# Two raw query-and-key buffers, later maxima and ten GpSimd pauses in an attention and feed-forward kernel

## The chip, the cores and the metric

One core of one Trainium2 chip runs the whole program. The metric is the device time of one execution in microseconds. On the core, PE (TensorE) multiplies matrices, DVE (VectorE), ACT (ScalarE) and POOL (GpSimd) work on elements, and SP (SyncE) issues the DMA transfers. Each engine does its own instructions strictly in order.

## The reference

```python
def _attn_ref(q_l, k_l, v_l, q_g, k_g, v_g):      # batch 8, heads 8, 512 local + 32 global tokens, head_dim 64
    window, scale = 32, 1.0 / np.sqrt(D)
    k_all = np.concatenate([k_g, k_l], axis=2)
    v_all = np.concatenate([v_g, v_l], axis=2)
    out_g = np.matmul(sm(scale * np.matmul(q_g, k_all.transpose(0, 1, 3, 2))), v_all)
    s_ll = scale * np.matmul(q_l, k_l.transpose(0, 1, 3, 2))
    s_ll = np.where(np.abs(pos[:, None] - pos[None, :]) <= window, s_ll, -1000000000.0)
    s_lg = scale * np.matmul(q_l, k_g.transpose(0, 1, 3, 2))
    out_l = np.matmul(sm(np.concatenate([s_lg, s_ll], axis=-1)), v_all)
    return np.concatenate([out_g, out_l], axis=2)

def _moe_ref(x, w_in, w_out):                     # 4608 tokens x 512, d_ff 2048
    h = x @ w_in
    g = h * np.cos(h)
    return g @ w_out
```

`sm` is the softmax over the last axis; the attention's output, tokens by 512, is x. Everything is float32 in and out.

## The kernel before

**Planes.** The matmuls take float16. A float32 operand is scaled by a power of two, found from its largest magnitude, and kept as two float16 planes, a high one (the rounded value) and a low one (what is left). A product is three matmuls: high by high, high by low, low by high.

**Attention** runs by batch b (0 to 7) and pair p of heads (0 to 3). Batches 0 and 1 have a path of their own; batches 2 to 7 take these steps for a pair:

- `load_qk` (L505): SP loads the pair's raw queries and keys, 608 KB, into the tile `qkr`, of which there is one buffer.
- `qk_a`, `qk_b`, `qk_c`: DVE finds the largest magnitude `qm` (L584) and puts it on a diagonal `d_qk` (L560); PE spreads it over the partitions (`pm_qk`, L566); DVE makes the scale `qs` (L571) and the factor `al` (L603) of it.
- `qk_d`: ACT writes the high plane `qa` (L624), DVE the low plane `kl` (L625, 128x1216). After `kl` the buffer of `qkr` is free.
- `qk_e`: SP moves halves of the planes to where PE wants them (`kh` L634 and L635, `qa` L637, `kl` L639).
- scores: PE `ps` (L879, L880); DVE adds the mask and finds the minimum (`t` and `mn`, L896, one custom instruction, which also frees the PSUM buffer); ACT takes Exp (L484); DVE the sums' reciprocals `sm` (L915, L916); POOL normalizes `t` (L926) and makes the low plane `plx` (L931).
- SP transposes `plx` to `ptb` (L936), PE multiplies by the values (`acc`, L968), and ACT and DVE write the result's planes `xh` and `xl` (L987, L988). The global tokens have the like (`gps`, `gt`, `planes_g`, `gacc`).

Values go by batch: `load_v` (L553, 1280 KB into `vr`, one buffer), `v_a` (DVE `vm`, L653, one reduce over 128x2560, and a diagonal `d_v`), `v_b` and `v_c` (`pm_v` on PE, the scale on DVE), and by pair `v_d` (the planes `vhl`, ACT L682 and DVE L683).

**The feed-forward** runs in 16 chunks c of 256 tokens (two to a batch) and one of all global tokens, in 8 slots j each. For a slot: `m1_a` puts h into a PSUM tile `ph` (PE, L1126, three buffers); `m1_b` and `m1_c` reduce the angle (`u`, ACT L1148 and DVE L1149) and take the sine (ACT); `m1_d` squares it on POOL (`w`, L1163), multiplies by h on DVE (`gf`, L1165, which frees `ph`), and makes the planes `gh` (ACT, L1169) and `gl` (POOL, L1170); `m2_a` multiplies by w_out into `po` (PE, L1184 to L1186). After slot 7 `m2_b` writes `o` from `po`, one half on ACT and one on DVE (L1192), and `m2_c` stores it. `gh` and `gl` lie in a ring of `NG` = 11 buffers.

**The order.** Steps are put into lists by slot (`at`, 16 slots to a batch, offsets such as `s_load` and `s_vd`), and a scheduler orders each engine's instructions from there; `tc.add_manual_dep` adds a dependence that it must keep, with a semaphore (`sync`) or in the order alone (`order`).

```python
t = 16 * (b - 1) + T0[b > 2] + SH
tv = max(t + s_v, 19)
at(tv, PA0, load_v, b)
at(tv + 1, PF, v_a, b)
at(tv + (1 if b == 2 else 2), PG if b == 2 else PA, v_b, b)
at(tv + (1 if b == 2 else 2), PG2 if b == 2 else PB, v_c, b)
```

Of the kernel before, what the change touches and what calls it, by code (L numbers as in the profile page):

```python
# [15 lines left out]
ALU = mybir.AluOpType  # L16
AX = mybir.AxisListType
# [34 lines left out]
LAG = 6  # L52
NG = 11
MASK = -(2.0**120)
# [53 lines left out]
s_tr = -1  # L108
s_vd = -8
s_av = 0  # L110
# [36 lines left out]
def body(tc, qk, qkf, v, wi, wo, mask, out):  # L147
# [3 lines left out]
    with ExitStack() as ctx:  # L151
# [15 lines left out]
        planes = [plx[:, i] for i in range(4)]  # L167
        vhl = cp.tile([P, 2, 5, NT, P], F16, name="vhl")
        vhlf = vhl.rearrange("p a b c d -> p (a b c d)")
# [320 lines left out]
        def load_qk(b, p):  # L490
            if b in FB:
                if p > 0:
                    tag = ("qa", "kh", "kl")[p - 1]
                    q, k = (ap_.tile([P, NZ], F32, tag=tag, name=f"{n}f_{b}_{p}") for n in "qk")
                else:
                    t = ap_.tile([P, 2, NZ], F32, tag="qkr", name=f"qkr_{b}_{p}", bufs=1)
                    q, k = t[:, 0], t[:, 1]
                st["qkf", b, p] = (q, k)
                if b:
                    load_half(b, p, 0, NZ)  # L500
                else:
                    load_half(b, p, 0, ZH)
                return
            t = ap_.tile([P, 2, NZ], F32, tag="qkr", name=f"qkr_{b}_{p}", bufs=1)
            nc.sync.dma_start(t, qk[b, p])  # L505
            st["qkr", b, p] = t

        def h_load(b, p):
            if p > 0:
                tag = ("qa", "kh", "kl")[p - 1]  # L510
                q, k = (ap_.tile([P, NZ], F32, tag=tag, name=f"{n}f_{b}_{p}") for n in "qk")
            else:
                t = ap_.tile([P, 2, NZ], F32, tag="qkr", name=f"qkr_{b}_{p}", bufs=1)
# [55 lines left out]
        def scale_of(s, m):  # L569
# [4 lines left out]
            )  # L574

        def qk_a(b, p):
            m = ap_.tile([P, 1], F32, tag="qm", name=f"qm_{b}_{p}")

            if b < QMA:
                kl = ap_.tile([P, 2, NZ], F16, tag="kl", name=f"kl_{b}_{p}")  # L580
                st["kl", b, p] = kl
                nc.scalar.activation(kl.bitcast(BF16), st["qkr", b, p], AF.Abs, accum_out=m)
            else:
                nc.vector.tensor_reduce(  # L584
                    m, st["qkr", b, p], axis=AX.XY, op=ALU.max, apply_absolute_value=True
                )
            pow2(m, m)
            spread_a(m, 2.0**-40, f"qk{b}_{p}")
# [19 lines left out]
        def qk_d(b, p):  # L608
# [32 lines left out]
        def v_a(b):  # L641
            m = ap_.tile([P, 1], F32, tag="vm", name=f"vm_{b}")
            if b < QMA:
                m4 = ap_.tile([P, 4], F32, tag="vm4", name=f"vm4_{b}", bufs=1)
                for p in range(4):
                    o = 4096 + 640 * (p % 3)
                    nc.scalar.activation(
                        vhlf[:, o : o + 640].bitcast(BF16), st["vr", b][:, p].rearrange("p a b -> p (a b)"),
                        AF.Abs, accum_out=m4[:, p : p + 1],
                    )  # L650
                nc.vector.tensor_reduce(m, m4, axis=AX.X, op=ALU.max)
            else:
# [230 lines left out]
        def sc_b(b, p, i):  # L883
# [272 lines left out]
        def m1_d(c, j):  # L1156
# [319 lines left out]
```

## Time and profile before

| what | value |
|---|---|
| three runs | 1016.23, 1016.11, 1013.29 us; median 1016.11 |
| profiled execution, its own time | 1014.64 us |
| its span, first to last instruction | 1012.9 us |
| mean granted TensorE clock | 0.957 of full |
| busy: PE, DVE, ACT, POOL | 909.4, 652.7, 657.8, 644.5 us |
| chain that ended last, largest shares | PE 37%, POOL 14%, DMA 10%, DVE 9% |

The profile is of one execution. Busy times are sums over the span; a matmul's row can overlap the next one's, and what an engine waited for is inferred from the semaphore that released it. The 1.74 us between the span and its own time lie around the program.

### The profile page before, as it was taken

To read this page: it belongs to the slowest core of one execution; us is meant where nothing else is said; L and a number is where in the kernel's file an instruction comes from. 1 tells how busy PE (TensorE), PEld (TensorE's weight loads), DVE (VectorE), ACT (ScalarE), POOL (GpSimd) and SP (SyncE) were. 2 spreads that over 40 slices of the span, in tenths; PEclk is the share of its full clock that TensorE was granted. 3 is DMA by queue.
4 is the path that set the end of the run, shared out by engine and by line. 5 is a ranking of instruction groups with operands and counts; after the bars stand their busy time and mean duration, and the time that the engine had idled before them with its cause. 6 is when DMAs were issued, how large, how long until landed. Compare 5 with 4: busy or idle time off the path is not lost.

```text
span 1012.9 us, 20948 instructions
## 1 busy us (share of the span) xinstructions
PE 909.4 (90%) x7892; PEld 620.0 (61%) x7892; DVE 652.7 (64%) x1534; ACT 657.8 (65%) x1322; POOL 644.5 (64%) x862
## 2 busy tenths in 40 slices
PE   5659977887999789998999899989989999999996
PEld 4547644455666566765666566666657676666662
DVE  6998698567776777576677658586857553332230
ACT  4669886567788387766686677667767775434440
POOL 3457998745777577867677576747676877344440
PEclk9779995998999899999999999999999999999999
DMA  9684114646754465554546454545464523000000
GB/s 356 237 288 160 54 60 115 116 100 153 148 110 115 103 168 101 105 129 109 107 96 122 119 118 83 123 136 125 92 126 92 101 43 76 1 22 10 13 21 21
DMA packets 162254, 110.79 MB, mean 109 GB/s; under 512 B 140136, under 2 KB 142312, under 8 KB 160232
## 3 DMA queue, kind: packets, MB, share of 16 engines
q1 hardware_dynamic: 162152, 109.44, 43.9%
q8 instruction: 62, 1.02, 0.4%
q14 instruction: 40, 0.33, 0.1%
HBM read 51.61 MB, written 8.91 MB: 60 GB/s over the span
## 4 chain that ended last, share of the span: by engine, by line
PE 37%; POOL 14%; DMA 10%; DVE 9%; ACT 4%; issue 4%; SPq 1%; POOLq 0%; ACTq 0%; DVEq 0%
PE ph L1126 17%; POOL plx L931 6%; PE po L1184 6%; PE po L1186 6%; PE po L1185 5%; POOL t L926 4%; DMA qkr<-qk 4%; DMA vr<-v 2%; DVE kl L625 2%; POOL w L1163 2%; DMA ptb<-plx 2%; ACT t L484 1%; DVE qm L584 1%; POOL gl L1170 1%; PE acc L968 1%
## 5 line engine op out<-in xcount | busy, mean ns | idle before, releaser
L1126 PE MATMUL ph<-xh,wi_h 128*128 128x256 f16 x1024 | 283.3, 278 | 28.2 <-DVE gf L1165 23.6
L1126 PE MATMUL ph<-xl,wi_h 128*128 128x256 f16 x1024 | 283.5, 277 | 0.9 <-DVE xl L805 0.9
L1126 PE MATMUL ph<-xh,wi_l 128*128 128x256 f16 x1024 | 283.5, 277 | 0.0
L1126 PEld LDWEIGHTS <-wi_h 128*128 128x128 f16 x2176 | 213.2, 99 | 78.8 <-issue 33.7
L1170 POOL TENSOR_TENSOR gl<-gf,gh 128x512 f16<-128x512 f32 x136 | 159.9, 1176 | 124.3 <-ACT gh L1169 124.3
L1184 PE MATMUL po<-wo_h,gh 128*128 128x512 f16 x544 | 208.1, 384 | 5.7 <-DVE o L1192 4.9
L1185 PE MATMUL po<-wo_l,gh 128*128 128x512 f16 x544 | 208.1, 383 | 0.7 <-POOL wo_l L236 0.7
L1186 PE MATMUL po<-wo_h,gl 128*128 128x512 f16 x544 | 207.5, 383 | 0.0
L1163 POOL TENSOR_TENSOR w<-w 128x512 f32<-128x512 f32 x136 | 144.5, 1064 | 90.5 <-ACT w L484 90.2
L1149 DVE SCALAR_TENSOR_TENSOR u<-u,cm,ph 128x512 f32<-128x512 f32 x136 | 101.0, 743 | 118.2 <-ACT u L1148 118.0
L1165 DVE SCALAR_TENSOR_TENSOR gf<-w,ph 128x512 f32<-128x512 f32 x136 | 92.9, 683 | 106.5 <-POOL w L1163 106.4
L1169 ACT CAST gh<-gf 128x512 f16<-128x512 f32 x136 | 83.0, 611 | 118.6 <-DVE gf L1165 117.6
L484 ACT ACTIVATE t<-t,mn 128x224 f32<-128x224 f32 (+1 forms) x256 | 117.7, 461 | 58.8 <-DVE mn L896 40.9
L926 POOL TENSOR_TENSOR t<-t,sm 128x192 f32<-128x192 f32 (+1 forms) x192 | 101.9, 563 | 71.1 <-DVE sm L916 71.1
L484 ACT ACTIVATE w<-u,ca 128x512 f32<-128x512 f32 x136 | 97.5, 720 | 63.3 <-DVE u L1149 59.6
L931 POOL TENSOR_TENSOR plx<-t,plx 128x192 f16<-128x192 f32 (+1 forms) x192 | 118.3, 646 | 0.0
L1126 PEld LDWEIGHTS <-wi_l 128*128 128x128 f16 x1088 | 108.1, 99 | 15.5 <-issue 1.3
L1148 ACT ACTIVATE u<-ph,cm 128x512 f32<-128x512 f32 x136 | 92.0, 678 | 23.7 <-PE ph L1126 23.6
L1186 PEld LDWEIGHTS <-gl 128*128 128x128 f16 x544 | 53.7, 99 | 63.9 <-issue 4.1
L1185 PEld LDWEIGHTS <-gh 128*128 128x128 f16 x544 | 53.6, 99 | 60.5 <-issue 11.2
L1184 PEld LDWEIGHTS <-gh 128*128 128x128 f16 x544 | 53.7, 99 | 52.2 <-issue 2.8
L896 DVE CUSTOM_DVE_ANT_0 t<-ps,msk,al 128x192 f32<-128x192 f32 (+1 forms) x192 | 75.6, 427 | 8.1 <-PE ps L880 8.1
(235 smaller groups left out, 1374.0 us busy)
## 6 DMA issues: line engine op xcount, KB each, us to landing
qkr<-qk SPq DMA_DIRECT2D x24, 608.0 KB, 4.7
vr<-v SPq DMA_DIRECT2D x8, 1280.0 KB, 8.4
out<-o SPq DMA_DIRECT2D x34, 256.0 KB, 2.0
kh<-qa SPq DMA_DIRECT2D x48, 152.0 KB, 2.7
wo_h<-wo SPq DMA_DIRECT2D x8, 512.0 KB, 5.2
wo_l<-wo SPq DMA_DIRECT2D x8, 512.0 KB, 5.5
qa<-kl SPq DMA_DIRECT2D x24, 152.0 KB, 3.2
kl<-kl SPq DMA_DIRECT2D x24, 152.0 KB, 3.0
```

The lines of the kernel that those rows point to most:

```text
L484: ins = nc.scalar.activation(*a, **k).ins
L926: nc.gpsimd.tensor_tensor(t[:, h], t[:, h], rb[:, h], op=ALU.mult)
L931: nc.gpsimd.tensor_tensor(lo[:, h], t[:, h], hi[:, h], op=ALU.subtract)
L1126: nc.tensor.matmul(ph[:, a], w[:, kc, f], x[:, kc, q], start=first and ip == 0, stop=last and ip == 2, skip_group_check=True,)
L1148: nc.scalar.activation(u, ph, AF.Identity, bias=m)
L1149: nc.vector.scalar_tensor_tensor(u, u, m, ph, op0=ALU.subtract, op1=ALU.subtract)
L1163: nc.gpsimd.tensor_tensor(w, w, w, op=ALU.mult)
L1165: nc.vector.scalar_tensor_tensor(gf, w, 0.5, st.pop(("ph", c, j)).rearrange("p a b -> p (a b)"), op0=ALU.subtract, op1=ALU.mult,)
L1170: nc.gpsimd.tensor_tensor(gl, gf, gh, op=ALU.subtract)
L1184: nc.tensor.matmul(po[k], gh[:, q], wo_h[:, f], start=(f == 0), stop=False)
L1185: nc.tensor.matmul(po[k], gh[:, q], wo_l[:, f], start=False, stop=False)
L1186: nc.tensor.matmul(po[k], gl[:, q], wo_h[:, f], start=False, stop=(f == NJ - 1))
```

## The change

1. `qkr` has two buffers (the tile pool's default). A dependence in the order alone (`held`) puts `qm` of a pair behind `kl` of the pair before on DVE. Batch 1's raw loads are spread over other tiles (`h_load`).
2. The ring `NG` of `gh` and `gl` has 10 buffers.
3. The value planes `vhl` have four buffers, one to a pair, where there were five, and `s_vd` goes from -8 to -6, so that they are written two slots later.
4. For b > 2 `v_q` takes the place of `v_a`, three slots later: four reduces of 128x640 into `vm4` and one over their results, each held behind a `t` instruction of the last pair of the batch before. `v_b` and `v_c` come three slots later too.
5. `port_gap`: in slot 7 of chunks 2 to 11, POOL's `w` waits on a semaphore for `kl` of pair 2c + 8 (counted over all batches), which is pair 0 or 2 of a batch.

```diff
-NG = 11
+NG = 10
-s_vd = -8
+s_vd = -6
-        vhl = cp.tile([P, 2, 5, NT, P], F16, name="vhl")
+        vhl = cp.tile([P, 2, 4, NT, P], F16, name="vhl")
+        def port_gap(ins, key):
+            if key in st:
+                tc.add_manual_dep(ins, st[key].name, sync, reason="port_gap")
...
 def load_qk(b, p):
-            t = ap_.tile([P, 2, NZ], F32, tag="qkr", name=f"qkr_{b}_{p}", bufs=1)
+            t = ap_.tile([P, 2, NZ], F32, tag="qkr", name=f"qkr_{b}_{p}")
...
 def h_load(b, p):
-            if p > 0:
-                tag = ("qa", "kh", "kl")[p - 1]
-                q, k = (ap_.tile([P, NZ], F32, tag=tag, name=f"{n}f_{b}_{p}") for n in "qk")
+            if p > 1:
+                tags = (("kl", "kl"), ("qa", "kh"))[p - 2]
+                q, k = (ap_.tile([P, NZ], F32, tag=t, name=f"{n}f_{b}_{p}") for n, t in zip("qk", tags))
...
+        def held(ins, key):
+            if key in st:
+                tc.add_manual_dep(ins, st[key].name, order, reason="place")
 def qk_a(b, p):
-                nc.vector.tensor_reduce(
+                ins = nc.vector.tensor_reduce(
                     m, st["qkr", b, p], axis=AX.XY, op=ALU.max, apply_absolute_value=True
-                )
+                ).ins
+                held(ins, ("klins", NPAIR * b + p - 1))
...
+        def v_q(b):
+            m = ap_.tile([P, 1], F32, tag="vm", name=f"vm_{b}")
+            m4 = ap_.tile([P, 4], F32, tag="vm4", name=f"vm4_{b}", bufs=1)
+            for p in range(NPAIR):
+                ins = nc.vector.tensor_reduce(
+                    m4[:, p : p + 1], st["vr", b][:, p], axis=AX.XY, op=ALU.max,
+                    apply_absolute_value=True,
+                ).ins
+                held(ins, ("tins", b - 1, VPIN, p))
+            nc.vector.tensor_reduce(m, m4, axis=AX.X, op=ALU.max)
+            spread_a(m, 2.0**-100, f"v{b}")
...
 def m1_d(c, j):
-            nc.gpsimd.tensor_tensor(w, w, w, op=ALU.mult)
+            ins = nc.gpsimd.tensor_tensor(w, w, w, op=ALU.mult).ins
+            if j == 7 and c > 1:
+                port_gap(ins, ("klins", 2 * c + 8))
...
-            at(tv + 1, PF, v_a, b)
-            at(tv + (1 if b == 2 else 2), PG if b == 2 else PA, v_b, b)
-            at(tv + (1 if b == 2 else 2), PG2 if b == 2 else PB, v_c, b)
+            at(tv + (1 if b == 2 else 2 + 2), PF, v_a if b == 2 else v_q, b)
+            at(tv + (1 if b == 2 else 3 + 2), PG if b == 2 else PA, v_b, b)
+            at(tv + (1 if b == 2 else 3 + 2), PG2 if b == 2 else PB, v_c, b)
```

How instructions move, at three places. The numbers behind a name are batch and pair, or chunk and slot, and last a running number; the change's line numbers are some 5 to 26 higher.

DVE in the second pair of batch 5, before: the maximum of batch 6's values (`vm_6`).

```order
L584 TENSOR_REDUCE qm_5_3_7409<-qkr_5_3_7309 128x1
L206 TENSOR_SCALAR qm_5_3_7409<-qm_5_3_7409 128x1
L560 TENSOR_SCALAR d_qk5_3_7412<-ident_64,qm_5_3_7409 128x128
L1149 SCALAR_TENSOR_TENSOR u_8_1_7344<-u_8_1_7344,cm_8_7239,ph_8_1_7319 128x512
L653 TENSOR_REDUCE vm_6_7881<-vr_6_7707 128x1
L896 ISA t_5_1_2_7304,mn_5_1_3_7402<-ps_5_1_3_7397,msk_73,al_5_1_6711 128x192
L896 ISA mn_5_1_3_7402 128x1
L896 ISA t_5_1_2_7304,mn_5_1_3_7402<-ps_5_1_3_7397,msk_73,al_5_1_6711 128x192
L896 ISA mn_5_1_3_7402 128x1
L988 SCALAR_TENSOR_TENSOR xl_5_7406<-acc_5_0_7360,xs_91,xh_5_7405 128x512
L915 TENSOR_SCALAR sm_5_1_7416<-sm_5_1_7416 128x8
```

DVE in the change, where that maximum now stands, in the last pair of batch 5:

```order
L920 ISA t_5_3_2_8090,mn_5_3_3_8188<-ps_5_3_3_8183,msk_73,al_5_3_7501 128x192
L920 ISA mn_5_3_3_8188 128x1
L920 ISA t_5_3_2_8090,mn_5_3_3_8188<-ps_5_3_3_8183,msk_73,al_5_3_7501 128x192
L920 ISA mn_5_3_3_8188 128x1
L674 TENSOR_REDUCE vm4_6_8194<-vr_6_7721 128x1
L1012 SCALAR_TENSOR_TENSOR xl_5_7420<-acc_5_2_8146,xs_91,xh_5_7419 128x512
L939 TENSOR_SCALAR sm_5_3_8207<-sm_5_3_8207 128x8
L679 TENSOR_REDUCE vm_6_8193<-vm4_6_8194 128x1
L1057 TENSOR_SCALAR gsm_5_1_8216<-gsm_5_1_8216 128x1
L940 RECIPROCAL sm_5_3_8207<-sm_5_3_8207 128x8
L565 TENSOR_SCALAR d_v6_8200<-ident_64,vm_6_8193 128x128
```

The one long reduce stood ahead of the scores of the second pair; the four short ones stand behind the score instructions of the fourth pair (the last of them, `vm4_6`, is shown), and `vm_6` is over four numbers only.

DVE at the start of batch 6, before:

```order
L1015 COPY gal_6_0_8636<-al_6_1_8270 64x1
L1165 SCALAR_TENSOR_TENSOR gf_9_1_8213<-w_9_1_8128,ph_9_1_8102 128x512
L625 SCALAR_TENSOR_TENSOR kl_6_1_8362<-qkr_6_1_8092,qs_6_1_8265,qa_6_1_8361 128x1216
L1149 SCALAR_TENSOR_TENSOR u_9_3_8336<-u_9_3_8336,cm_8_7239,ph_9_3_8311 128x512
L896 ISA t_6_0_1_8357,mn_6_0_1_8358<-ps_6_0_1_8352,msk_73,al_6_0_7847 128x224
L896 ISA mn_6_0_1_8358 128x1
L896 ISA t_6_0_1_8357,mn_6_0_1_8358<-ps_6_0_1_8352,msk_73,al_6_0_7847 128x224
L896 ISA mn_6_0_1_8358 128x1
L1165 SCALAR_TENSOR_TENSOR gf_9_2_8307<-w_9_2_8243,ph_9_2_8217 128x512
L1149 SCALAR_TENSOR_TENSOR u_9_4_8399<-u_9_4_8399,cm_8_7239,ph_9_4_8374 128x512
```

and in the change, from the same `gf_9_1` on:

```order
L1191 SCALAR_TENSOR_TENSOR gf_9_1_8223<-w_9_1_8131,ph_9_1_8105 128x512
L1173 SCALAR_TENSOR_TENSOR u_9_3_8353<-u_9_3_8353,cm_8_7253,ph_9_3_8328 128x512
L707 SCALAR_TENSOR_TENSOR vhl_77<-vr_6_7721,vs_6_8277,vhl_77 128x640 x2
L920 ISA t_6_0_1_8374,mn_6_0_1_8375<-ps_6_0_1_8369,msk_73,al_6_0_7859 128x224
L920 ISA mn_6_0_1_8375 128x1
L1191 SCALAR_TENSOR_TENSOR gf_9_2_8324<-w_9_2_8253,ph_9_2_8227 128x512
L920 ISA t_6_0_1_8374,mn_6_0_1_8375<-ps_6_0_1_8369,msk_73,al_6_0_7859 128x224
L920 ISA mn_6_0_1_8375 128x1
L635 SCALAR_TENSOR_TENSOR kl_6_1_8381<-qkr_6_1_8095,qs_6_1_8282,qa_6_1_8380 128x1216
L593 TENSOR_REDUCE qm_6_2_8556<-qkr_6_2_8452 128x1
L1173 SCALAR_TENSOR_TENSOR u_9_4_8418<-u_9_4_8418,cm_8_7253,ph_9_4_8393 128x512
```

The two `vhl` planes have come in ahead of `kl_6_1`, `kl_6_1` stands one `gf` later than it did, and `qm_6_2` follows it at once, where before it came seven rows behind the last row shown.

POOL at the end of chunk 8, before:

```order
L1163 TENSOR_TENSOR w_8_6_7809<-w_8_6_7809 128x512
L1170 TENSOR_TENSOR gl_8_5_7777<-gf_8_5_7779,gh_8_5_7776 128x512
L931 TENSOR_TENSOR plx_76<-t_5_2_2_7647,plx_76 128x224 x2
L931 TENSOR_TENSOR plx_76<-t_5_2_2_7647,plx_76 128x192 x2
L1163 TENSOR_TENSOR w_8_7_7919<-w_8_7_7919 128x512
L1170 TENSOR_TENSOR gl_8_6_7887<-gf_8_6_7889,gh_8_6_7886 128x512
L1170 TENSOR_TENSOR gl_8_7_8029<-gf_8_7_8031,gh_8_7_8028 128x512
```

and in the change:

```order
L1187 TENSOR_TENSOR w_8_6_7821<-w_8_6_7821 128x512
L1196 TENSOR_TENSOR gl_8_5_7789<-gf_8_5_7791,gh_8_5_7788 128x512
L955 TENSOR_TENSOR plx_76<-t_5_2_2_7661,plx_76 128x224 x2
L955 TENSOR_TENSOR plx_76<-t_5_2_2_7661,plx_76 128x192 x2
L1196 TENSOR_TENSOR gl_8_6_7895<-gf_8_6_7897,gh_8_6_7894 128x512
L1187 TENSOR_TENSOR w_8_7_7927<-w_8_7_7927 128x512
L1196 TENSOR_TENSOR gl_8_7_8032<-gf_8_7_8034,gh_8_7_8031 128x512
L1187 TENSOR_TENSOR w_9_0_8064<-w_9_0_8064 128x512
```

`w_8_7`, which now waits for the low plane of batch 6's first pair (2 x 8 + 8 = 24 = 4 x 6 + 0), has moved behind `gl_8_6`.

On SP the loads of `qkr` stand one pair earlier: those of batch 2's pairs 0 and 1 follow each other, and the load of `vr` comes next; before, that of pair 1 came only behind the moves of pair 0's `kh`. The raw queries and keys of batch 1's first pair are loaded ahead of the pieces of w_out.

## Rows read from the trace of the kernel before

**Rows 1.** Busy time in stretches of the span. Columns: the stretch, its length, busy us (and instructions) of PE, PEld, DVE, ACT and POOL, the granted TensorE clock (1.00 is full), the DMA engines' busy share, GB/s.

```profile
270.00:380.00 110.00, 97.92 (x917) 68.05 (x915) 79.95 (x191) 78.20 (x168) 75.92 (x101) 0.94 0.57 129
380.00:450.00 70.00, 70.00 (x692) 48.35 (x691) 49.86 (x122) 50.01 (x98) 52.21 (x72) 1.00 0.50 98
450.00:773.00 323.00, 302.00 (x2821) 207.82 (x2820) 226.29 (x539) 224.80 (x462) 221.30 (x294) 0.99 0.51 115
```

**Rows 2.** PE's waits between 450 and 773 us by line: what it waited for; us in total, times, longest.

```profile
PE pm_qk L566 <- DVE mn L896: 8.2, 3, 2.9
PE po L1184 <- DVE o L1192: 4.9, 5, 1.9
PE ph L1126 <- DVE gf L1165: 4.2, 9, 0.6
PE gacc L1059 <- DVE mn L896: 2.2, 3, 0.7
PE acc L968 <- DMA ptb<-plx: 1.1, 1, 1.1
```

**Rows 3.** Single starts on PE with a wait before them. Columns of this and the other timelines: start us, duration us, engine, line, operation, out<-in, shape, count, and in brackets the idle time before it and what ended that.

```profile
463.21 0.22 PE L566 MATMUL pm_qk<-d_qk,ones 128*128 128x128 bf16 x1 [2.41 <-DVE mn L896]
...
470.50 0.27 PE L1126 MATMUL ph<-xh,wi_h 128*128 128x256 f16 x1 [0.61 <-DVE gf L1165]
...
488.33 0.38 PE L1184 MATMUL po<-wo_h,gh 128*128 128x512 f16 x1 [1.31 <-DVE o L1192]
```

**Rows 4.** DVE's waits for loads between 380 and 830 us, columns as in the waits above.

```profile
DVE qm L584 <- DMA qkr<-qk: 20.6, 11, 3.4
...
DVE vm L653 <- DMA vr<-v: 3.5, 3, 1.6
```

**Rows 5.** DVE's timeline around a batch's first steps (459 to 488 us).

```profile
459.67 2.82 DVE L653 TENSOR_REDUCE vm<-vr 128x1 f32<-128x2560 f32 x1 [1.13 <-DMA vr<-v]
462.40 0.41 DVE L896 CUSTOM_DVE_ANT_0 t<-ps,msk,al 128x192 f32<-128x192 f32 x1
...
484.96 1.42 DVE L584 TENSOR_REDUCE qm<-qkr 128x1 f32<-128x1216 f32 x1 [2.64 <-DMA qkr<-qk]
...
487.53 0.74 DVE L1192 TENSOR_SCALAR o<-po,co 128x512 f32<-128x512 f32 x1
```

**Rows 6.** The chain of waits between 445 and 490 us, its two loads: start, duration, what.

```profile
451.76 7.88 DMA vr<-v
...
479.77 5.17 DMA qkr<-qk
```

**Rows 7.** SP's timeline (it issues the loads; a row is the issue, not the transfer).

```profile
231.67 0.38 SPq L553 DMA_DIRECT2D vr<-v  x1
...
233.36 0.47 SPq L634 DMA_DIRECT2D kh<-qa  x1
...
235.90 0.35 SPq L505 DMA_DIRECT2D qkr<-qk  x1
```

**Rows 8.** PE's waits between 230 and 380 us, columns as above.

```profile
PE ph L1126 <- DVE gf L1165: 8.0, 4, 5.6
PE ps L879 <- DMA qa<-kl: 5.1, 1, 5.1
PE ps L880 <- DMA kl<-kl: 2.6, 1, 2.6
```

**Rows 9.** The chain of waits between 236 and 262 us, its two transfers: start, duration, what.

```profile
233.88 6.41 DMA kh<-qa
...
240.35 2.35 DMA qa<-kl
```

**Rows 10.** All executions of line 625: count, shortest/median/longest ns, first and last start.

```profile
L625 DVE SCALAR_TENSOR_TENSOR kl<-qkr,qs,qa x24: 1467/1863/8524, 216.0 to 790.8; 128x1216 f16<-128x1216 f32 x24
```

**Rows 11.** DVE's timeline, three of those executions.

```profile
332.79 8.52 DVE L625 SCALAR_TENSOR_TENSOR kl<-qkr,qs,qa 128x1216 f16<-128x1216 f32 x1
...
445.40 4.04 DVE L625 SCALAR_TENSOR_TENSOR kl<-qkr,qs,qa 128x1216 f16<-128x1216 f32 x1
...
470.83 1.86 DVE L625 SCALAR_TENSOR_TENSOR kl<-qkr,qs,qa 128x1216 f16<-128x1216 f32 x1 [0.39 <-ACT qa L624]
```

**Rows 12.** POOL's timeline around the first two of these, and the long run of work at a batch's start.

```profile
338.98 1.05 POOL L931 TENSOR_TENSOR plx<-t,plx 128x192 f16<-128x192 f32 x2
...
443.86 2.20 POOL L931 TENSOR_TENSOR plx<-t,plx 128x224 f16<-128x224 f32 x4
446.01 1.05 POOL L1163 TENSOR_TENSOR w<-w 128x512 f32<-128x512 f32 x1
447.00 1.16 POOL L1170 TENSOR_TENSOR gl<-gf,gh 128x512 f16<-128x512 f32 x1
451.76 1.16 POOL L1170 TENSOR_TENSOR gl<-gf,gh 128x512 f16<-128x512 f32 x1 [3.60 <-ACT gh L1169]
...
464.36 4.36 POOL L926 TENSOR_TENSOR t<-t,sm 128x192 f32<-128x192 f32 x8 [5.95 <-DVE sm L916]
...
480.56 1.04 POOL L1163 TENSOR_TENSOR w<-w 128x512 f32<-128x512 f32 x1
```

**Rows 13.** Busy time in one stretch, columns as in rows 1.

```profile
464.36:481.60 17.24, 16.01 (x122) 10.54 (x121) 10.64 (x28) 12.92 (x25) 17.24 (x23) 1.00 0.59 113
```

**Rows 14.** The page's sixth part: a DMA issue, its engine and count, KB each, us from issue to landing.

```profile
qkr<-qk SPq DMA_DIRECT2D x24, 608.0 KB, 4.7
```

More of the change, by code (lines that the diff above doesn't have):

```diff
@@ L46 @@
 HB = (1,)
+VPIN = 3
 FTE = ((1, 1, 0, 1), (0, 0, 0, 0))
@@ L503, in load_qk @@
                 return
-            t = ap_.tile([P, 2, NZ], F32, tag="qkr", name=f"qkr_{b}_{p}", bufs=1)
+            t = ap_.tile([P, 2, NZ], F32, tag="qkr", name=f"qkr_{b}_{p}")
             nc.sync.dma_start(t, qk[b, p])
@@ L508, in h_load @@
         def h_load(b, p):
-            if p > 0:
-                tag = ("qa", "kh", "kl")[p - 1]
-                q, k = (ap_.tile([P, NZ], F32, tag=tag, name=f"{n}f_{b}_{p}") for n in "qk")
+            if p > 1:
+                tags = (("kl", "kl"), ("qa", "kh"))[p - 2]
+                q, k = (ap_.tile([P, NZ], F32, tag=t, name=f"{n}f_{b}_{p}") for n, t in zip("qk", tags))
             else:
-                t = ap_.tile([P, 2, NZ], F32, tag="qkr", name=f"qkr_{b}_{p}", bufs=1)
+                t = ap_.tile([P, 2, NZ], F32, tag="qkr", name=f"qkr_{b}_{p}")
                 q, k = t[:, 0], t[:, 1]
@@ L624, in qk_d @@
                 nc.scalar.activation(qa, t, AF.Identity, scale=s)
-                nc.vector.scalar_tensor_tensor(kl, t, s, qa, op0=ALU.mult, op1=ALU.subtract)
+                st["klins", NPAIR * b + p] = nc.vector.scalar_tensor_tensor(
+                    kl, t, s, qa, op0=ALU.mult, op1=ALU.subtract
+                ).ins
             kh = ap_.tile([P, 2, NZ], F16, tag="kh", name=f"kh_{nm}")
@@ L645, in v_a @@
                 for p in range(4):
-                    o = 4096 + 640 * (p % 3)
+                    o = 4096
                     nc.scalar.activation(
@@ L655, in v_a @@
                 )
+            spread_a(m, 2.0**-100, f"v{b}")
[6 more added lines that the diff above has]
+                    apply_absolute_value=True,
+                ).ins
+                held(ins, ("tins", b - 1, VPIN, p))
+            nc.vector.tensor_reduce(m, m4, axis=AX.X, op=ALU.max)
             spread_a(m, 2.0**-100, f"v{b}")
@@ L673, in v_d @@
             t, s = st["vr", b], st["vs", b]
-            vh, vl = (vhl[:, i, (NPAIR * b + p) % 5] for i in range(2))
+            vh, vl = (vhl[:, i, p] for i in range(2))
             ve = VE[min(b, 2)]
@@ L895, in sc_b @@
             for h in range(2):
-                nc.vector.tensor_tensor_reduce(
+                st["tins", b, p, i] = nc.vector.tensor_tensor_reduce(
                     t[:, h], pt[:, h], msk[:, MOFF[i] : MOFF[i] + w], al, 3.0e38,
                     ALU.add, ALU.min, mn[:, h : h + 1],
-                )
+                ).ins
             st["t", b, p, i] = (t, mn)
```

## The prediction

> **What bounds the kernel now.** I read the busy times by stretch first. Between 380 and 450 us PE is busy all 70.00 us at full clock, while DVE, ACT and POOL are busy for about 50 each [rows 1]: there the matmuls set the time and the elementwise work fits beside them. The kernel can gain only where PE stands still or is throttled. Between 450 and 773 us PE is busy for 302.00 of 323.00 us [rows 1], so 21.0 us are idle at a granted clock of 0.99. Between 270 and 380 us it is 97.92 of 110.00.
>
> The second view is PE's waits. The five rows of 450 to 773 us sum to 20.6 us, nearly the whole idle time [rows 2]. Largest is `pm_qk`: 8.2 us in three waits, one to each batch start in the stretch. The reader should not stop at the name of the releaser. `pm_qk` needs a PSUM buffer that the score instruction `t` frees; `t` starts at 462.40 because DVE, which works in order, is held by `vm` until then: 1.13 us of waiting for the values' load, then 2.82 us of reducing [rows 5]. PE resumes at 463.21 after 2.41 us [rows 3]. The waits of `po` for `o` have the same form: `o` at 487.53 stands behind `qm` at 484.96, which had waited 2.64 us for its load [rows 5], and PE lost 1.31 us [rows 3].
>
> The third view, DVE's own waits, tells how common this is: `qm` waits 20.6 us in 11 times between 380 and 830 us, `vm` 3.5 us in three [rows 4]. The chain of waits holds both loads, 7.88 and 5.17 us [rows 6]: with one `qkr` buffer a load can only start once `kl` has read the old data.
>
> **The change part by part.** The sum is made against the profiled execution's own 1014.64 us, 1.47 us below the median of the three runs (1016.11). A measurement of this kernel tells about 0.3%, 3 us, from no change.
>
> *1. The maximum of the values.* It leaves the place ahead of the first pairs' scores; four short reduces go behind the last pair's scores. Load wait and reduce no longer stand between PE and a PSUM buffer: **-8.2 us** [rows 2]. The reducing itself stays, 2.82 us a batch, about 0.7 us a piece [rows 5]; a piece could hold up the next `pm_qk` in each of three batches, 3 x 0.7 = 2.1, so the weak end is -6.1. I take the full amount, since DVE has room: 226.29 busy of 323.00 us [rows 1].
>
> *2. The second `qkr` buffer.* A load is issued one pair, about a quarter of a batch, ahead; on SP it waits for `kl` of two pairs before, long done, so nothing queues behind it there. The longest wait of `qm` is 3.4 us [rows 4] and a load takes 4.7 us [rows 14], so a whole pair covers it. What was behind `qm` on DVE gets free: of the 4.9 us of `po` I take **-4.0** (ends 0 and -4.9), since I followed the mechanism through one of the five waits only.
>
> *3. POOL's late start.* At a batch's start POOL idles 5.95 us for `sm`, which comes after `vm` on DVE, then works without a break from 464.36 to 481.60: 17.24 of 17.24 us [rows 12, 13]. `ph` waits for `gf` in such a run, 0.61 us at 470.50 [rows 3]. An earlier `sm` starts the run earlier. Of the row's nine waits I take four of this size, two to a batch start: 4 x 0.6 = **-2.4** (ends 0 and -4.2, the whole row [rows 2]).
>
> *4. The pauses.* `kl` at 445.40 took 4.04 us; the shortest of the 24 took 1.467 [rows 10, 11]. It ended at 449.44, 1.28 us after POOL's `gl` had ended at 448.16; on POOL `plx`, `w` and `gl` had followed each other without a gap [rows 12]. At 332.79 it took 8.52 us, until 1.28 us after POOL's last `plx` of that run (340.03) [rows 11, 12]. So `kl` can stand still for as long as POOL's queue is full, and a pause lets it in. In the steady part a hold of 4.04 - 1.47 = 2.57 us shows no wait on PE of its own: between 380 and 450 us, with 445.40 inside, PE was never idle [rows 1]. There the pause gains nothing. The 8.52 us one cost PE 5.6 us [rows 8]; there the pausing `w` is one of the last instructions of POOL's run, so I take a third, **-1.9** (ends 0 and -5.6). The price: `w` waits up to 1.47 us for `kl`, ten times, 14.7 us at most, and `gf`, `gh` and `gl` queue behind it. I take 0: POOL idled 3.60 us right behind [rows 12], and holds of 2.57 us on DVE, on which the same `gf` stands, cost nothing. That slack is the cover; gone, the ten pauses would cost up to those 14.7.
>
> By the Trainium skill (SBUF — State Buffer, section "SBUF: two separate sides") a DVE operation with two SBUF inputs and GpSimd contend for one port pair, which whichever starts first holds for one whole instruction. By that rule `kl` would get in when the running POOL instruction ends, at most about 1.2 us later. The trace differs: `kl` stood through several ends, and the measurement decides. By the rule, this term and the next would both be near 0, and the sum -16.6 instead of -15.5; it would also strike rival C below.
>
> *5. Batch 3's load.* At 231.67 SP issues the 1280 KB of `vr`, then `kh`, then `qkr` at 235.90 [rows 7]; `kh` needs 6.41 us [rows 9], and PE waits 5.1 us for `qa` and 2.6 us for `kl` [rows 8]. In the change `qkr` goes ahead of these, `vr` stays. One of two competitors leaves: **-2.0** of the 5.1 (ends 0 and -5.1).
>
> *6. What moves into POOL's dense run.* Two `vhl` instructions and the odd pairs' `kl` of five batches now fall into it, where `kl` before mostly got away with 1.86 us [rows 11]. Two holds of up to 2.57 us in five batches are 25.7 us of DVE time. On PE a hold of 2.57 showed 0 and one of 7.05 (8.52 - 1.47) 5.6, so the ends are 0 and 5 x 5.6 = 28. The nearest row is the 2.57 us hold, but in the dense run `gf` is already late by 0.61 [rows 3]; I take one such wait to a batch, 5 x 0.6 = **+3.0**.
>
> *7. At no cost.* The ring of 10: no wait of PE, DVE or POOL in the rows is for a buffer of `gh` or `gl`; with slots of some 6.7 us (323 us in three batches of 16) the one buffer less is one slot of reserve out of eleven. If that cover is gone, `gh` and then POOL wait for `po`. Four `vhl` planes: each is written two slots later, so none waits for its old reader. The batch-1 load ahead of w_out's pieces: one load, 0 to 4.7 us [rows 14], beside work that doesn't need it; I take 0.
>
> Sum: -8.2 - 4.0 - 2.4 - 1.9 - 2.0 + 3.0 = -15.5, so 1014.64 - 15.5 = **999 us**. Next in line are `gacc`'s waits (2.2 us) and what is left of `gf`'s [rows 2].
>
> **The rivals.**
>
> *A, more than the sum.* If all idle time of the steady part goes (20.6), and in the transition 5.6, 5.1 and 2.6 too [rows 2, 8], it is -33.9, 981 us; half of the surplus gives 990. For it: with DVE, ACT and POOL about 70% busy there, nothing else is near its limit [rows 1]. Against: POOL's run stays dense.
>
> *B, the pauses give it back.* The removed waits are worth 15.5, and `w` late ten times by 1.47 us costs 14.7: about 1014. It decides if `ph`'s three buffers are already all in use when the pause comes. For it: `ph` waits for `gf` nine times [rows 2]. Against: those waits lie in the dense run, the pauses at the end of a chunk, before POOL's 3.60 us idle. Here belongs, too, that `kl` misses the pause, because `qa` is late, and POOL waits for nothing.
>
> *C, slower: the moved work is caught by the dense run.* On DVE the two `vhl` and then `kl` come up in the run of 17.24 us. If they are held not for 2.57 us but to the run's end, `gf` stands behind them and PE stops, as behind the 8.52 us `kl`. Five times 5.6 in place of term 6's 3.0 gives 1014.64 - 18.5 + 28 = 1024 us. It loses against before from 18.5 / 5 = 3.7 us on PE a batch; between the two holds known (2.57 us: 0, 7.05 us: 5.6) that is a hold of about 5.5 us. For it: by both rows a full POOL queue holds DVE without limit. Against: the odd `kl` at 470.83 lay in the run and took only 1.86 us [rows 11], so the run has places where it gets in.
>
> **How the numbers follow.** The forecast has a chance of 0.52; its own range is 992 (terms 1 to 4 at their full ends, -22.9, the others 0) to 1007 (term 1 at -6.1, 2 to 5 at half, 6 at +3: -8.2). A has 0.17, B 0.16, C 0.15. The range of 984 to 1014 takes in most of A and all of B's middle, and leaves out C and a little of A and B. Faster by over 0.3% are the forecast, A and a third of B: 0.74. Within 0.3% is most of B: 0.11. Slower is C: 0.15.
>
> **What would show it.** Right: no wait of `qm` for `qkr` and none of `vm` for `vr` on DVE; `pm_qk` gone from PE's waits; PE's idle time over three steady batches down from 21 us to some 7; even pairs' `kl` at about 1.5 us instead of 4.04, with POOL idle before slot 7's `w`. Term 6 is read from the odd `kl` and the first two `vhl` of a batch: about 4 us is the forecast, over 7 us with PE waits of 4 us for `gf` is C. The prediction is wrong if PE's idle time stays at 21 us under other names, or if `ph` waits for `gf` right after each pause (B).

## The result, and the profile after

The changed kernel takes 999.22 us (median of four, 995.87 to 999.53) against 1016.17 of before: 0.9833 of the time, 95% interval 0.9805 to 0.986. The profiled execution took 999.00; 999.0 was forecast. The sum hides two errors of some 6 us that cancel, as this section and the experiments show.

First, where the time went. DVE's `o` of a chunk's second half marks a chunk's end in every profile (its start in the timeline, us):

| chunk | before | change | difference | change, second profile |
|---|---|---|---|---|
| 0 | 185.59 | 187.39 | +1.80 | +2.36 |
| 1 | 231.82 | 237.04 | +5.22 | +5.10 |
| 3 | 374.02 | 375.19 | +1.17 | +0.91 |
| 4 | 432.06 | 435.51 | +3.45 | +3.17 |
| 7 | 594.20 | 587.32 | -6.88 | -7.18 |
| 11 | 805.21 | 789.45 | -15.76 | -16.02 |
| 16 | 1003.70 | 987.92 | -15.78 | -15.90 |

Chunk 2 is left out: its end comes 11 to 20 us later than before in every other kernel of this document, the one with the smaller ring and four planes alone among them, while chunk 3's end is at most 9 us later, so it is no common mark. Up to chunk 4 the change loses 3.4 us, from there to chunk 11 it gains 19.2, and after that nothing. That middle part, called the steady part below, in busy time (columns as in [rows 1]), first before:

```profile
432.06:805.21 373.15, 351.47 (x3288) 241.99 (x3286) 260.10 (x625) 261.16 (x538) 257.67 (x343) 1.00 0.51 112
```

and the changed kernel:

```profile
435.51:789.45 353.94, 346.89 (x3286) 241.21 (x3286) 250.26 (x638) 263.63 (x541) 259.42 (x344) 1.00 0.53 117
```

PE's idle time falls from 21.7 to 7.1 us. All of PE's waits there in the change, to be held against [rows 2]:

```profile
PE po L1210 <- ACT o L1220: 3.5, 3, 1.3
PE acc L992 <- DMA ptb<-plx: 1.7, 2, 1.4
PE ph L1150 <- DVE gf L1191: 1.6, 3, 0.7
PE ps L904 <- DMA kl<-kl: 1.1, 1, 1.1
```

In this stretch the five rows of [rows 2] had 8.2, 4.9, 4.4, 2.2 and 1.4 us before. Those of `pm_qk` and `gacc` are gone, and `gf`'s has shrunk from 4.4 to 1.6. `po` no longer waits for DVE's half of `o` but for ACT's, which stands behind a row of Exp, so on that line only 1.4 us of 4.9 are won. PE's busy time is 4.6 us lower too, for the same matmuls. Some 1.7 us of that is clock: before, PE ran at half clock for part of the stretch from 570 us on, behind the 2.90 us wait of the second `pm_qk`:

```profile
570.00:575.00 5.00, 4.74 (x27) 3.35 (x27) 3.62 (x11) 4.97 (x11) 3.58 (x7) 0.66 0.01 3
```

A granted mean of 0.66 over 5 us is 1.7 us of lost work. In the change no slice of 5 us in the steady part is below 1.00. The rest of the 4.6 I can't name.

DVE's waits in the change from 380 to 830 us answer to [rows 4]:

```profile
DVE u L1173 <- ACT u L1172: 89.0, 49, 3.7
DVE gf L1191 <- POOL w L1187: 44.7, 47, 3.0
DVE t L920 <- PE ps L904: 1.9, 1, 1.9
DVE gsm L1057 <- ACT gt L489: 1.6, 5, 0.3
DVE kl L635 <- ACT qa L634: 1.5, 4, 0.4
```

No load is waited for any more, neither by `qm` nor by the values' maximum: DVE idles at `u` and `gf` instead, whose inputs come from PE's `ph` by way of ACT and POOL. The short reduces stand as they were placed, one behind each pair of score instructions (timeline of DVE):

```profile
492.88 0.41 DVE L920 CUSTOM_DVE_ANT_0 t<-ps,msk,al 128x192 f32<-128x192 f32 x1
493.22 0.82 DVE L674 TENSOR_REDUCE vm<-vr 128x1 f32<-128x640 f32 x1
...
513.02 0.82 DVE L674 TENSOR_REDUCE vm<-vr 128x1 f32<-128x640 f32 x1
514.48 0.15 DVE L679 TENSOR_REDUCE vm<-vm 128x1 f32<-128x4 f32 x1
```

The low planes answer to [rows 10, 11]; all of line 635; then, in order of time, the two `vhl` in POOL's dense run, an odd pair in it, an even pair, two `vhl` outside the run, and an odd pair:

```profile
L635 DVE SCALAR_TENSOR_TENSOR kl<-qkr,qs,qa x24: 1479/1863/5451, 218.1 to 775.0; 128x1216 f16<-128x1216 f32 x24
```

```profile
522.66 2.63 DVE L707 SCALAR_TENSOR_TENSOR vhl<-vr,vs,vhl 128x640 f16<-128x640 f32 x2
526.55 1.63 DVE L635 SCALAR_TENSOR_TENSOR kl<-qkr,qs,qa 128x1216 f16<-128x1216 f32 x1
...
550.21 3.04 DVE L635 SCALAR_TENSOR_TENSOR kl<-qkr,qs,qa 128x1216 f16<-128x1216 f32 x1
...
554.70 1.67 DVE L707 SCALAR_TENSOR_TENSOR vhl<-vr,vs,vhl 128x640 f16<-128x640 f32 x2
...
572.36 1.86 DVE L635 SCALAR_TENSOR_TENSOR kl<-qkr,qs,qa 128x1216 f16<-128x1216 f32 x1 [0.39 <-ACT qa L634]
```

Even pairs take 3.04 us where 4.04 was and 1.5 was forecast; odd pairs 1.63 and 1.86, not the 4 us of term 6.

### The profile page after: what moved, and what is told of

Read it like the earlier page. It is cut to its first block, busy times and chain, and to the rows that moved or that the text cites. A ratio compares the mean times of both kernels' runs of the same rounds, so it can differ in the third digit from the quotient of the medians.

```text
span 997.1 us, 20954 instructions
## 1 busy us (share of the span) xinstructions
PE 905.9 (91%) x7892; PEld 616.6 (62%) x7892; DVE 642.7 (64%) x1554; ACT 658.3 (66%) x1322; POOL 644.7 (65%) x862
## 4 chain that ended last, share of the span: by engine, by line
PE 39%; ACT 14%; DVE 13%; POOL 5%; issue 3%; DMA 2%; SPq 1%; ACTq 0%; POOLq 0%; DVEq 0%
PE ph L1150 17%; PE po L1210 6%; PE po L1211 6%; PE po L1212 6%; ACT t L489 5%; DVE kl L635 3%; POOL t L950 2%; ACT L489 2%; DVE u L1173 2%; DVE qm L593 2%; ACT u L1172 2%; DVE t L920 2%; POOL plx L955 1%; PE acc L992 1%; ACT w L489 1%
## 5 line engine op out<-in xcount | busy, mean ns | idle before, releaser
L955 POOL TENSOR_TENSOR plx<-t,plx 128x192 f16<-128x192 f32 (+1 forms) x192 | 120.5, 658 | 0.0
L1150 PEld LDWEIGHTS <-wi_l 128*128 128x128 f16 x1088 | 107.8, 99 | 15.5 <-issue 1.3
```

The costliest lines, as they stand in the source:

```text
L955: nc.gpsimd.tensor_tensor(lo[:, h], t[:, h], hi[:, h], op=ALU.subtract)
L1150: nc.tensor.matmul(ph[:, a], w[:, kc, f], x[:, kc, q], start=first and ip == 0, stop=last and ip == 2, skip_group_check=True,)
```

## The experiments

Three parts can be put in and left out: **vm** (the later, split maximum of the values), **qkr** (the second buffer), **pause**. The smaller ring and the four planes pay for them. With the kernels below all eight combinations are measured. The stretch is the steady part in the one profile of each; the ratio is to the kernel before.

| parts beside ring and planes | ratio (95% interval) | steady part, us |
|---|---|---|
| kernel before, without ring and planes | 1 | 373.2 |
| none | 1.003 (1.0016 to 1.0044) | 370.2 |
| pause | 1.0001 (0.9987 to 1.0015) | 372.7 |
| qkr | 0.9946 (0.9931 to 0.9962) | 368.3 |
| vm | 0.9913 (0.9888 to 0.9937) | 363.2 |
| qkr, pause | 0.9935 (0.991 to 0.996) | 362.1 |
| vm, pause | 0.9906 (0.9878 to 0.9933) | 359.2 |
| vm, qkr | 0.9889 (0.9858 to 0.992) | 360.9 |
| all: the change | 0.9833 (0.9805 to 0.986) | 353.9 |

A difference between two of these ratios is good to some 2 to 4 us, by their intervals. Some of the stretches hold half clock; the work that PE lost by it there is 1.7 us in the kernel before, 3.4 with none of the parts, 3.4 with pause, 4.9 with qkr, 1.7 with qkr and pause, 1.7 with vm and qkr, and none in the other three.

**Without the pauses.**

```diff
-            if j == 7 and c > 1:
-                port_gap(ins, ("klins", 2 * c + 8))
```

> The changed kernel without GpSimd's ten pauses, all else as changed. Theory (the prediction's term 4): the pauses are worth nothing between 430 and 790 us and some 2 us around 340 us, so about 1001 us (999 to 1004), with the even pairs' low plane back at 4 us instead of 3.04 and no new wait of PE between 430 and 790 us. Rival P (the pauses are the lever): the low plane is held at the end of every second pair and the maximum of queries and keys, which now follows it directly, is late with it, so pm_qk or o are waited for again: 1007 us or more.

1003.6 us, ratio 0.9889: by the ratios some 5.7 us slower than the change, where the theory had about 2. The median lies in the theory's range all the same (999 to 1004) and short of the rival's 1007, but the theory's ground was wrong: the even pairs' `kl` is back at 4.04 us, and the steady part, where the pauses were to be worth nothing, takes 7.0 us more. At 566.82 PE has waited 2.55 us for the move of `kl` (the chain of waits):

```profile
548.64 4.04 DVE kl L635
...
556.26 10.51 DMA kl<-kl
566.77 0.04 issue
566.82 0.24 PE ps L904
...
567.28 4.29 PE ph L1150 x24
```

The move of 152 KB takes 10.51 us. SP had issued the 608 KB of `qkr` and the 1280 KB of `vr` just ahead of it; in the kernel below where `vr` comes behind it, the same move takes 3.23. The 24 matmuls behind the wait take 4.29 us, as the clock is halved again for part of the time (a mean of 0.66 over 5 us):

```profile
567.00:572.00 5.00, 5.00 (x31) 3.55 (x29) 3.40 (x13) 5.00 (x9) 5.00 (x8) 0.66 0.01 2
```

**One buffer of raw queries and keys.** `bufs=1` is put back, with the old tiles in `h_load`.

```diff
-            t = ap_.tile([P, 2, NZ], F32, tag="qkr", name=f"qkr_{b}_{p}")
+            t = ap_.tile([P, 2, NZ], F32, tag="qkr", name=f"qkr_{b}_{p}", bufs=1)
```

> The changed kernel with one buffer of raw queries and keys, all else as changed (later maximum of the values and pauses stay). Theory (terms 2 and 5): the waits of qm for its load come back (some 20 us on DVE), and PE gets back those of po for o (4.0) and the 2 us of batch 3's load: about 1005 us. Rival Q (the second buffer is the lever, since all that stands behind qm on DVE is late): 1010 us or more, with PE waits in the steady part near 20 us again. Rival V (only the maximum of the values counted): 999 us.

1004.76 us, the theory's figure; by the ratio, 0.9906, 7.4 us behind the change. `qm` waits for its load again, 27.9 us in the steady part, and PE gets back `po` for DVE:

```profile
PE ps L904 <- DMA kl<-kl: 2.4, 2, 1.8
PE ph L1150 <- DVE gf L1191: 2.2, 7, 0.6
PE acc L992 <- DMA ptb<-plx: 2.1, 2, 1.6
PE po L1210 <- DVE o L1218: 1.9, 2, 1.7
PE po L1210 <- DVE qm L207: 1.9, 3, 0.9
```

These are 3.8 us of `po`, against the 4.0 of term 2, but they stand in place of the 3.5 us for ACT's `o` that the change has: the line as a whole hardly differs. The steady part is 5.3 us longer, spread over `ps`, `ph` and other rows. Most of `qm`'s 27.9 us stay hidden.

**The values' maximum at the old place.**

```diff
-            at(tv + (1 if b == 2 else 2 + 2), PF, v_a if b == 2 else v_q, b)
-            at(tv + (1 if b == 2 else 3 + 2), PG if b == 2 else PA, v_b, b)
+            at(tv + 1, PF, v_a, b)
+            at(tv + (1 if b == 2 else 2), PG if b == 2 else PA, v_b, b)
...
```

> The changed kernel with the maximum of the values as before: one reduce, at the old slot. Theory (terms 1 and 3): PE's waits at pm_qk come back (8.2 us in three batches) and the late start of GpSimd's run (2.4): about 1010 us. Since the value planes are written two slots later than before, the values' load starts later too, so it may be more: up to 1015. Rival: with the second buffer pm_qk has been issued long before, so the reduce is hidden: 1001 us or less.

1007.09 us; the ratio 0.9935 puts it 10.4 us behind the change, the size of terms 1 and 3 together (10.6). PE's waits in the steady part show both, the 8.2 and 2.4 us of the forecast as 6.5 and some 2 (3.5 against 1.6):

```profile
PE pm_qk L571 <- DVE mn L920: 6.5, 3, 2.9
PE ph L1150 <- DVE gf L1191: 3.5, 5, 1.0
PE ps L904 <- DMA kl<-kl: 0.7, 2, 0.5
```

**Only the price.** The kernel before with `NG = 10`, four `vhl` planes and `s_vd = -6`.

> The kernel before with only what the change takes away: ten buffers in the g ring, four of value planes, these written two slots later. Theory (term 7): no cost, 1016 us within 3. Rival C7: this is what made the changed kernel's first four chunks slower (its chunk 4 ended 3.4 us later than before, chunk 1 5.2 us), so 1020 us or more, by the same amount at chunk 4's end.

Ratio 1.003, 3.0 us slower (1.6 to 4.5): neither the 0 of term 7 nor the rival's size. Its chunk 1 ended 3.69 us and chunk 4 7.70 us later than before, in a profile that was the slowest of its ten executions.

**Each part on that price.** `vm` alone and `qkr` alone are the kernels above with the other parts undone as well.

> The kernel before with the ten-buffer ring and the four value planes, and of the change only the later, split maximum of the values: one buffer of raw queries and keys, no pauses. Theory (parts add up: price +3 us as measured, terms 1 and 3 -10.4 us as the kernel without this part lost): 1009 us. Rival (the parts need each other: the maximum's place only pays when qm doesn't wait for its load): 1014 us or more. Either way pm_qk should be gone from PE's longest waits.

> The kernel before with the ten-buffer ring and the four value planes, and of the change only the second buffer of raw queries and keys with qm behind kl: the values' maximum as before, no pauses. Theory (parts add up: +3 us and -7.4 us): 1012 us; pm_qk's waits stay at some 7 us, qm's waits for its load are gone. Rival: without them PE is still held by vm, so nothing comes of it: 1017 us or more.

Ratios 0.9913 and 0.9946. Both theories' sums (7.4 and 4.4 us faster than before) lie in the intervals and both rivals' outside them; `pm_qk` is gone from PE's waits with vm, and stands at 8.8 us with qkr. By these ratios the parts bring 11.9 and 8.5 us over the price; together (vm, qkr) 14.3. So they overlap by some 6 us. My reading, which no run tests by itself, is that a place on DVE that waits for neither load is won once.

**Only the pauses.**

> The kernel before with the ten-buffer ring and four value planes, and of the change only the pauses (one buffer of raw queries and keys, the values' maximum as before). Chunk 4 to 11 took 370.3 us with the ring and planes alone, and the pauses took 4 to 7 us from it in the other pairs of profiles. Theory (they add up): 363 to 367 us, median some 1013 us. Rival I (by the medians pauses gave 1 us where only one of the other parts was there, so alone they give nothing): 370 us, 1016 to 1018 us. The prediction's term 4 said 0 in this stretch.

The steady part takes 372.7 us: rival I, there. PE's waits in it are those of before, here the first two rows:

```profile
PE pm_qk L571 <- DVE mn L920: 8.2, 3, 2.9
PE po L1210 <- DVE o L1218: 7.6, 7, 1.9
```

A low plane that is ready 1 us earlier is no use where `qm` and `vm` wait for loads behind it: `qm` waits 28.8 us there, and 24.1 without the pauses. The ratio of the whole, 1.0001, fits the rival's 1016 us too, but it is 2.9 us under the same kernel without pauses (1.003; the intervals just miss each other), so the rival's ground, that pauses alone give nothing, holds for the steady part only. By the profiles that gain lies ahead of chunk 4, which ends 1.6 us later than before, and 7.7 later with ring and planes alone.

In the steady part the pauses take 4.0 us off beside vm, 6.2 beside qkr, 7.0 beside both, and 2.5 us is added without either. Without what the half clock cost in each of these kernels it is 4.0, 3.0, 5.3 and again 2.5 added (beside both, the two kernels below with the other order of loads differ by 7.0, and neither has half clock there). By the ratios of the whole the pauses gain 0.7, 1.1, 5.7 and 2.9. Each stretch comes from one profile a kernel (two for the change). So both measures have the pauses worth most beside both parts; what they are worth beside one is not settled.

**Is it the move of `kl`?** The change without pauses, with the values' load ordered behind that move on SP:

```diff
-            nc.sync.dma_start(t, v[b])
+            held(nc.sync.dma_start(t, v[b]).ins, ("klmv", b - 1, 2))
...
-                move(kl[0:64], kl[64:128])
+                st["klmv", b, p] = move(kl[0:64], kl[64:128]).ins
```

> The changed kernel without pauses, and with the values' load behind the move of kl on SP. Without pauses chunk 4 to 11 took 361.0 us, with them 353.9. Theory K (most of what a pause gives is that the low plane is ready before the 1280 KB load takes the DMA engines: PE's 2.55 us wait for the move of kl and the half clock after it): the wait is gone, 357 us from chunk 4 to 11 and a median of 1001 us. Rival G (the pause works through DVE's freed time, gf and ph): 361 us again, 1003 to 1004 us.

Ratio 0.9894 (0.987 to 0.9919), steady part 360.9: rival G. The wait for `kl` is gone, the time is not. PE's waits in the steady part, first of this kernel, then of the change's second profile:

```profile
PE ph L1150 <- DVE gf L1189: 6.0, 11, 0.8
PE po L1208 <- ACT o L1218: 2.2, 2, 1.3
PE acc L992 <- DMA ptb<-plx: 2.2, 3, 1.5
PE pm_v L571 <- DVE d_v L565: 1.2, 3, 0.4
```

```profile
PE po L1210 <- ACT o L1220: 3.8, 3, 1.3
PE acc L992 <- DMA ptb<-plx: 2.1, 2, 1.6
PE ph L1150 <- DVE gf L1191: 2.0, 4, 0.7
```

`ph` for `gf` makes 4.0 of the 6.9 us. Another 2.4 are busy time of PE. So a pause works mainly through DVE: what stands behind `kl` there, `gf` among it, comes earlier. POOL's timeline shows why that costs POOL nothing, in the change:

```profile
550.31 0.55 POOL L955 TENSOR_TENSOR plx<-t,plx 128x192 f16<-128x192 f32 x1
550.82 1.16 POOL L1196 TENSOR_TENSOR gl<-gf,gh 128x512 f16<-128x512 f32 x1
553.33 1.04 POOL L1187 TENSOR_TENSOR w<-w 128x512 f32<-128x512 f32 x1 [1.36 <-DVE kl L635]
557.75 1.16 POOL L1196 TENSOR_TENSOR gl<-gf,gh 128x512 f16<-128x512 f32 x1 [3.38 <-ACT gh L1195]
```

and at the same pair in the first kernel of this section, without pauses:

```profile
550.24 1.15 POOL L1194 TENSOR_TENSOR gl<-gf,gh 128x512 f16<-128x512 f32 x1
557.11 1.21 POOL L1194 TENSOR_TENSOR gl<-gf,gh 128x512 f16<-128x512 f32 x1 [5.72 <-ACT gh L1193]
```

POOL idles 5.72 us without the pause, and 1.36 + 3.38 = 4.74 with it. It would have waited for `gh`, and so for DVE, anyway; waiting earlier makes that wait shorter. The same holds over all of them: between 290 and 760 us nine of the ten pauses held POOL, 12.3 us in all, and its waits for `gh` come to 67.4 us, against 85.1 with the pauses left out and this order of loads.

**Pauses only from chunk 6 on** (`c > 5` for `c > 1`).

> The changed kernel with pauses from chunk 6 on only (six of ten). From the two profiles: without any pause chunk 4 ended 3.6 us earlier than with them, and from there on the kernel lost 7 us. Theory T (pauses cost in the transition and pay later): chunk 4 ends as without pauses, and the whole takes 996 us or less. Rival S (what is lost at chunk 4 is only put off, the totals before chunk 6 are alike): 999 us within 2. Rival U (the early pauses pay, as the prediction's term 4 had it): 1001 us or more.

Ratio 0.9846 (0.9809 to 0.9884): not told apart from the change, which fits rival S but doesn't show it. The four runs lie from 992.89 to 1000.26, and the profiled one was the fastest, so where its chunk 4 ends (428.46) says little.

**The change with that order of loads.** The edit of the kernel above, with the pauses.

> The changed kernel with one more dependence in the order alone: the load of a batch's values stands on SP behind the move of kl of the last batch's third pair. In the kernel without pauses that move took 10.51 us behind the 1280 KB load and PE waited 2.55 us and then ran at half clock for some 5 us. Theory L (order on SP decides): PE's waits for kl (1.1 and 0.6 us in the changed kernel) go, 997 to 998 us. Rival: the load comes too late for the four reduces, or nothing is gained since only 1 us of waiting is there: 999 us or more.

Ratio 0.9843 (0.9811 to 0.9876), median 996.35: not told apart either. The waits for `kl` are gone, but they were 1.1 us.

**The change again.**

> The changed kernel once more, unaltered, for a second profile. From the eight profiles so far, the time from chunk 4's to chunk 11's last o on DVE goes by what a kernel contains (373.2 us before, 353.9 to 355.0 in the three with all parts and the later pauses), while where chunk 4 ends varies by 11 us between kernels that differ in nothing there. Theory W (the transition scatters from execution to execution, the steady part does not): chunk 4 to 11 again 354 us within 1, and chunk 4's end some other place than 435.5. Rival: chunk 4 ends at 435.5 within 1, so that place belongs to the kernel. Median 997 to 1000 us either way.

997.97 us, ratio 0.9834. Theory W falls: chunk 4 ends at 435.23, the steady part takes 353.96 us, against 435.51 and 353.94. What is lost ahead of chunk 4 is the same in these two executions. But their totals are alike too, 999.00 and 998.81 us, near the slow end of what the kernel took (995.65 to 999.80), so that a faster execution loses as much there isn't shown.

**Both halves of `o` on DVE** (`OV = 3`).

> The changed kernel with both halves of o written by DVE (before one by ACT). In the changed kernel the largest of PE's waits from 430 us on is po for ACT's o, 3.5 us in three, as ACT has a row of Exp ahead of it. Theory A: DVE is free there, the waits go, chunk 4 to 11 in 351 us and a median of 996 us. Rival: DVE holds the next o as long, or gf and t behind it come later: 354 us or more, 999 us or more.

Ratio 0.9878 (0.985 to 0.9906), slower than the change by 4.6 us. The steady part takes 354.5 us, though `po` hardly waits there now:

```profile
PE acc L992 <- DMA ptb<-plx: 2.0, 2, 1.5
PE ph L1150 <- DVE gf L1191: 1.5, 3, 0.8
PE po L1210 <- DVE o L1218: 0.2, 1, 0.2
```

Of the 354.5 us, 1.7 are half clock at the start of the stretch, so the theory's 351 is missed by less than it seems. Most of the loss lies ahead of that: chunk 4 ends 3.7 us later than in the change, and between 230 and 440 us PE waits 9.1 us for `gf`, 4.7 in the change, and 4.8 for `ptb`, 1.6 in the change; the waits for `o` are shorter there too, 4.0 against 6.1. None of the runs gives a version that is clearly better than the change.

## Why the prediction was right, and where it was not

**Total.** -15.5 us forecast, -15.6 measured between the profiled executions. By place the sum was -12.8 in the steady part (terms 1 to 3, and 1.8 of term 6) and -2.7 ahead of it; measured were -19.2 and +3.4. That the total came out within 0.2 us is luck. Without the pauses the steady part is 12.2 us shorter than before (373.2 to 360.9 us), for the forecast's 12.8; what is missing in the sum there is the pauses' 7.0. PE's idle time fell from 21.7 to 7.1 us, the forecast's 21 to 7, but without the pauses it stood at 11.0.

**Terms 1 and 3** held in mechanism: that `pm_qk` waits for a PSUM buffer behind `vm` is shown by taking `vm` away and putting it back. In size they agree where the rest of the change stays, 10.6 forecast and 10.4 lost; but that includes what the pauses no longer bring when this part is gone. Without pauses the same part is worth 5.8 us beside qkr (0.9946 to 0.9889) and 11.9 alone. **Term 2** was half right: DVE's `o` is no longer waited for, 4.9 us, but 3.5 us for ACT's `o`, which the prediction didn't have, came in on the same line, so 1.4 were won there instead of 4.0. Instead `gacc`'s 2.2 us went, which the sum had left out as next in line.

**Term 4 is the step that failed.** The hold of 2.57 us at an even pair was priced at nothing, because PE never idled around 445.40 [rows 1]. That was true of the steady part before, where DVE lost its time to loads soon after, and the kernel with the pauses alone confirms it there. With both waits gone the same 1 us at each of seven even pairs is worth 7.0 us in the steady part. I priced a part in the old kernel that the other two parts make worth most. Rival B's ground, that `w` late by 1.36 us costs PE, is refuted: POOL waits less for `gh` in return, and PE's waits for `gf` are 1.6 us in three.

The mechanism of the term stands: with the pause `kl` takes 3.04 us, which is 1.6 us more than the shortest, held by the `plx` and `gl` already in POOL's queue; the forecast had some 1.5 us, that is no hold. The end of `plx` at 550.86, between the two, did not let it in. So the rule weighed in the prediction (the Trainium skill, SBUF — State Buffer, section "SBUF: two separate sides") is not borne out here either. (What the prediction works out from that rule, -16.6, sets terms 4 and 6 to 0; its words "this term and the next" would be terms 4 and 5.)

**Term 6** was too dear: the two `vhl` take 2.63 us together where the two outside the run take 1.67, and the odd `kl` 1.6 to 1.9. With no wait of `qm` behind them little of the 3.0 us can be left on PE: all its waits for `gf` in three batches are 1.6 us. Rival C is refuted by the same rows.

**Terms 4 and 5 in the transition** came out as a sum: from chunk 1's end to chunk 3's the change takes 138.15 us, before 142.20, so -4.1 for a forecast of -3.9. Singly they don't: without the pauses this stretch is 4.3 us longer than in the change, with one buffer 6.3, in one profile each, so how the -4.1 is divided is not shown. The waits of 5.6 and 5.1 us [rows 8] are gone, and the longest `kl` is 5.45 us where 8.52 was; new is `po` for ACT's `o`, 3.6 us at most, as PE's waits from 237 to 375 us show:

```profile
PE po L1210 <- ACT o L1220: 4.9, 2, 3.6
PE ph L1150 <- DVE gf L1191: 4.5, 3, 1.7
PE ps L903 <- ACT w L489: 1.5, 1, 1.5
PE ps L904 <- DMA kl<-kl: 1.2, 1, 1.2
```

**Term 7** was not 0. Ring and planes cost 3.0 us by the runs; which of the three edits does is open. Up to chunk 1's end the change is 5.2 us behind. The kernels with one raw buffer and ring and planes were 0.8, 1.5, 1.8 and 3.7 us behind there, those with two 3.6 to 6.6. So some 3 us go with the second buffer and the loads moved for it; within the 0 to 4.7 given, but I had taken 0. The 2.3 us lost from chunk 3 to 4 stay open. In three of the four pairs of kernels that differ in the pauses and have vm or qkr, chunk 4 ends 2.9 to 3.6 us later with them, in the fourth (with the other order of loads) 3.7 earlier; so the pauses may have a part in it, or not. The forecast's own range ends at 1006.4 by its sum (1014.64 - 8.2), not at 1007; that changes nothing.

## What to carry to other kernels

Price a change's parts together where they stand on the same engine's queue: here a shorter instruction was worth nothing in the steady part while the next one waited for a load, and some 1 us each time, its full length, once the loads were early. The other way round, two parts that free the same queue brought 20.4 us singly and 14.3 together. And a total that comes out right proves little: compare by stretch, at marks that both kernels share.

## What the runs showed of the hardware

In the steady part PE fell to half clock in or behind waits of 2.90 us before, 2.55 without pauses, 2.43 and 2.11 with ring and planes alone, 2.90 and 2.94 with the pauses alone, 2.86 with the values' maximum at the old place, 2.90 and 2.95 with the second buffer alone, and with both halves of `o` on DVE behind three short ones in a row (0.41, 1.15 and 0.68 us). Not every such wait brought it: behind the 2.41 us at 463.21 [rows 3] and 2.88 us at 678.93, both before, the clock stayed at 1.00. So the length of a single wait doesn't tell. A fall cost some 1.7 us on top of the wait: 24 matmuls in 4.29 us, where they take 2.62 at full clock.

The steady part repeats: 353.94 and 353.96 us in two executions of the same program. Its totals range over 4 us from run to run; that the steady part doesn't share in this is suggested by the change with the other order of loads, which took 353.92 us there in an execution of 994.44, but a fast execution of the change itself was not profiled.
